# Another order of work in the opening of a fused FNet and GeGLU kernel, and other places for three kinds of transfer in its last stage

## The chip, the cores and the metric

The kernel runs on one core of a Trainium2 chip. The core has a matrix engine (TensorE, PE in the profile; its weight loads are shown apart as PEld), a vector engine (VectorE, DVE), a scalar engine (ScalarE, ACT), a general engine (GpSimd, POOL) and SyncE (SP), which only issues transfers. Each of the first four works through its own instructions in the order in which they were written. The metric is the device time of one execution in microseconds; lower is better.

## The reference

```
xn = (x - mean) / sqrt(var + eps)             # x: 2048 rows of 448, statistics by row
a  = xn @ Wd_re.T ;  b = xn @ Wd_im.T         # hidden transform, 448 x 448
s  = Ws_re @ a - Ws_im @ b                    # sequence transform, 2048 x 2048
h  = gelu(xn @ w_gate) * (xn @ w_up)          # 448 x 1792 each
g  = silu(h @ w_down)                         # 1792 x 448
y  = x + s * g
```

All inputs are fp32. The kernel splits each fp32 operand into a high part (rounded to the format that the matrix engine takes, fp32r) and a low part (the difference), and adds three products: high by high, high by low, low by high. So nearly every operand costs a copy by ScalarE (the high part) and a subtraction by VectorE (the low part).

## The kernel before

The 2048 rows are 4 chunks of 512, a chunk is 4 row tiles of 128. The kernel has four stages.

**Opening.** For each row tile: VectorE takes the statistics (`one`, L154: bn_stats and bn_aggr), ScalarE and VectorE turn them into a factor (`root` and `newton`, L158 to L170), VectorE normalizes (`norm`, L172), TensorE turns the tile over (`turn_mm`, four transposes into one PSUM bank of two that take turns), and `turn_split` (L196) empties that bank: ScalarE copies the high part (L199), ScalarE copies the plain fp32 values to `xf` (L201, kept for the Strassen sums), VectorE subtracts to get the low part (L202). Between these TensorE multiplies the first weight blocks (`first`, L544, with 256 columns at a time; `gu_mm`, L353; `gateup`) and multiplies back (`down`, L406 to L433). `act` (L382) is the Gelu and the product: Gelu by ScalarE (L386), product by VectorE (m, L389), high part by ScalarE (h, L390), low part by VectorE (l, L391). Four sums per pair of chunks and side (`combine`, L207) prepare the Strassen products: for chunks 0 and 1 on VectorE, for chunks 2 and 3 on GpSimd. `t_places` and `v_places` split those sums, `prep_s` splits the summed weights that `sums_s` made on GpSimd.

**Strassen units** (`strassen`, L447; its products at L438 and L445): 24 units of matmuls, two weight blocks by two chunks each, with the multiplications back (`send`) in between; VectorE and ScalarE work through lists (`preps`) at four places of a unit. In the first units these lists also hold what is left of the splits of the chunks' sums.

**Hidden transform** (`hid_mm`): 16 row tiles; 14 of the results are kept as sums of halves (`TS`, seven blocks of 448 columns each), and four of these are also written to device memory as `td`.

**Last stage**, the loop at the end of `fnet_geglu`: for each of eight pairs of output row tiles 14 units of 14 matmuls (`seven`, L1113 and L1116, seven products by two) and two plain units (`plain`, L1128 to L1130). Two kept tiles are exchanged in each pair: unit 0 and unit 1 free a place each, and the loop loads the tiles that units 12 and 13 need into them, in four parts each, at the units that `LOAD_AT` names (L1180). `load_c` fetches the sequence matrices five units ahead, on SP (L1005) and with a second part on POOL (L1006); VectorE sums (L1012, L1013) and splits them (ScalarE L142, VectorE L143). In unit 13 and after it `gather` takes the seven products out of PSUM into the buffer `cc`: ScalarE one (L1136), VectorE seven (L1138 to L1144). In the next pair VectorE multiplies by the gate (L1151), POOL adds x by an accumulating transfer (L1153), and SP stores the two result tiles from `cc` at the units of `STORE_AT` (L1155). The last pair has its own places for loads (`LAST_AT`), and VectorE does all its additions (L1193 to L1229).

Everything is placed by hand: the order of the source is the order on each engine and each queue, and the framework adds the waits that the data, the buffers and the PSUM banks need. What an engine or a queue waits for holds up all that is written behind it there.

Of the kernel before, what the change touches and what calls it, by code (L numbers as in the profile page):

```python
# [10 lines left out]
AF = mybir.ActivationFunctionType  # L11
# [34 lines left out]
def fnet_geglu(ctx: ExitStack, tc: tile.TileContext, x, ca, ct, cp, et, wgu, wd, out):  # L46
# [102 lines left out]
    def stats(c, k0, n):  # L149
        st = const.tile([P, 4, 6], F32, name=f"st{c}_{k0}", tag="st", bufs=2)  # L150
        mv = const.tile([P, 4, 2], F32, name=f"mv{c}_{k0}", tag="mv", bufs=3)
        sd = const.tile([P, 4, 4], F32, name=f"sd{c}_{k0}", tag="sd", bufs=3)

        def one(i):  # L154
            nc.vector.bn_stats(st[:, i], xr[c][:, k0 + i, :D])
            nc.vector.bn_aggr(mv[:, i], st[:, i])

        def root():  # L158
            r, t, w = sd[:, :n, 0], sd[:, :n, 1], sd[:, :n, 2]
            nc.scalar.activation(t, mv[:, :n, 1], AF.Sqrt, bias=epst)  # L160
            nc.vector.tensor_scalar(w, mv[:, :n, 1], EPS, -0.5, op0=ALU.add, op1=ALU.mult)
            nc.vector.tensor_scalar_mul(sd[:, :n, 3], mv[:, :n, 0], -1.0)

        def newton():
            r, t, w = sd[:, :n, 0], sd[:, :n, 1], sd[:, :n, 2]
            nc.vector.reciprocal(r, t)

            nc.vector.tensor_mul(t, r, r)
            nc.vector.tensor_mul(t, t, w)
            nc.vector.scalar_tensor_tensor(r, t, 1.5, r, op0=ALU.add, op1=ALU.mult)  # L170

        def norm(i, eng=nc.vector):  # L172
            v = xr[c][:, k0 + i]
            if eng is nc.scalar:
                eng.activation(v, v, AF.Identity, bias=sd[:, i, 3:4])
                eng.activation(v, v, AF.Copy, scale=sd[:, i, 0:1])
            else:
                eng.tensor_scalar(
                    v, v, mv[:, i, 0:1], sd[:, i, 0:1], op0=ALU.subtract, op1=ALU.mult
                )  # L180

        return one, root, newton, norm
# [13 lines left out]
    def turn_split(c, k, pt):  # L196
        sl = slice(k * P, (k + 1) * P)
        h, l = [cols_of(xs(c, lo), c, sl) for lo in range(2)]
        nc.scalar.activation(h, turned(pt, c), AF.Copy)  # L199
        for i, v in enumerate(xf[c]):  # L200
            nc.scalar.activation(v[:, :, sl], pt[:, 3 * i :] if i else pt[:, : v.shape[1]], AF.Copy)  # L201
        nc.vector.tensor_sub(l, turned(pt, c), h)  # L202
# [313 lines left out]
    with tc.manual_schedule():  # L516
# [82 lines left out]
        one, root, newton, norm = stats(1, 0, 4)  # L599
        one(0)  # L600
        one(1)
        turn_split(*t2)
        turn_split(*t3)
        one(2)
        one(3)
# [6 lines left out]
        first(1, half[1], ("hh", "hl"))  # L612
        t0, t1 = turn_mm(1, 0), turn_mm(1, 1)
        first(1, half[1], ("lh", "last"))
        turn_split(*t0)
        turn_split(*t1)
# [4 lines left out]
        d_low()  # L621
# [5 lines left out]
        turn_split(*t2)  # L627
        turn_split(*t3)
        one(1)
        m0, h0, l0 = act(0, 0, pgs[0])  # L630
        m1, h1, l1 = act(1, 0, pgs[1])
# [8 lines left out]
        l1()  # L640
        newton()
        norm(0)
        norm(1)
        gu_mm(pg[0], ws[0], 0, 1, half[1], True)
# [8 lines left out]
        turn_split(*turn_mm(2, 0))  # L653
# [15 lines left out]
        comb = combine(0, 0, nc.vector) + combine(0, 1, nc.vector)  # L669

        def turn2(k):
            turn_split(*turn_mm(2, k))
            if k == 1:
                l0()
            comb.pop(0)()
# [6 lines left out]
        one(1)  # L682
        m1()
        h1()
        one(2)
        one(3)
        root()
        l1()
        newton()
        norm(0)  # L690
        norm(1)

# [3 lines left out]
        for c in (2, 3):  # L696
# [4 lines left out]
            m0, h0, l0 = gateup(0, c, ws[0])  # L701
            if c == 2:
                turn = lambda k: turn_split(*turn_mm(3, k))
                between = [
                    lambda: (m0(), h0(), norm(2)),
                    lambda: (l0(), norm(3), turn(0), comb.pop(0)()),
                    lambda: (turn(1), comb.pop(0)()),
                    lambda: (turn(2), comb.pop(0)()),
                ]
                between1 = [lambda: (turn(3), comb.pop(0)())]  # L710
            else:
                t_split = t_places(0)
                between = [
                    lambda: (m0(), v_split(2)),
# [4 lines left out]
                between1 = [lambda: v_split(0), lambda: v_split(3)]  # L719
            down(0, c - 1, wdn, between)  # L720
            if c == 2:
                nws[0], steps = prep_s(0, s_raw)
                for f in steps:
                    f()
            m1, h1, l1 = gateup(1, c, ws[1], between1)
            m1()
            if c == 2:
                h1()
                l1()
                comb.pop(0)()  # L730
                v_split = v_places(0)
                v_split(1)
# [54 lines left out]
        for gi in range(1, len(GROUPS)):  # L787
# [7 lines left out]
            for bi, (i, p) in enumerate(zip((0, 1, 1, 0), sides)):  # L795
                preps = [[], [], [], []]
                if gi == 1 and bi == 0:
                    for f in combine(1, 1, nc.gpsimd) + combine(1, 0, nc.gpsimd):
                        f()
                    tsp, vsp = t_places(1), v_places(1)  # L800
                    preps[0].append(lambda: vsp(3))
                    preps[3].append(lambda: (vsp(1), tsp(1)))
                if gi == 1 and bi == 1:
                    for n, f, k in ((0, tsp, 2), (1, vsp, 2), (2, tsp, 0), (3, vsp, 0)):
                        preps[n].append(lambda f=f, k=k: f(k))
                if gi == 1 and bi == 2:
                    tsp(3)
# [290 lines left out]
        LOAD_AT = 2, 3, 4, 5, 6, 7, 8, 9  # L1098
        LAST_AT = 2, 2, 3, 4, 5, 6, 7, 8
        STORE_AT = 5, 8  # L1100
# [208 lines left out]
```

## Time and profile before

| | |
|---|---|
| median of 3 runs (lowest to highest) | 774.27 us (773.34 to 774.31) |
| profiled execution: time, span | 775.69 us, 773.9 us |
| mean granted TensorE clock | 0.999 |
| busy, share of the span: PE / PEld / DVE / ACT / POOL | 99% / 89% / 71% / 47% / 25% |
| matmuls | 4044 |
| moved by DMA | 170.05 MB, 220 GB/s |

The busy time of PE counts each matmul from its start to its modelled end, and successive matmuls overlap. A short stall between two of them therefore hardly shows as idle time; it shows in the distance between their starts.

### The profile page before, as it was taken

The numbers are of one execution on the slowest core, as the hardware profiler recorded it, in microseconds if no ns is written. First come the engines' busy times: TensorE is split into PE (matmuls) and PEld (weight loads), VectorE is DVE, ScalarE is ACT, GpSimd is POOL, SyncE is SP. The second block draws the span as 40 slices with busy tenths as digits, with TensorE's granted clock in tenths as the row PEclk, the third lists the DMA queues.
The fourth block names the chain that finished last, engine by engine and source line by source line (L and its number), as shares of the span: only waits on it lengthen the run. The fifth ranks groups of instructions, "written<-read, shape, count | busy, mean of one in ns | idle before, by whom it ended". The sixth has DMA issues, their size and how long they took to land.

```text
span 773.9 us, 11384 instructions
## 1 busy us (share of the span) xinstructions
PE 763.9 (99%) x4044; PEld 686.2 (89%) x4044; DVE 546.6 (71%) x937; ACT 363.7 (47%) x538; POOL 189.8 (25%) x308
## 2 busy tenths in 40 slices
PE   8999999999999999999999999999999999999997
PEld 7888888888888888888889999999899999999996
DVE  7789867555556555456452767888788797979787
ACT  3885545434444344344444585544344444434341
POOL 1109133340511511501011001223132322313130
PEclk9999999999999999999999999999999999999999
DMA  8232557994969958875979972869696969697794
GB/s 296 89 119 89 205 200 159 266 188 90 271 116 242 275 114 221 175 157 87 265 210 248 376 319 71 272 222 320 204 335 190 360 194 360 205 310 235 275 289 173
DMA packets 61370, 170.05 MB, mean 220 GB/s; under 512 B 7424, under 2 KB 40064, under 8 KB 60416
## 3 DMA queue, kind: packets, MB, share of 16 engines
q1 hardware_dynamic: 47440, 108.17, 39.6%
q0 software_dynamic: 13728, 61.02, 34.4%
q8 instruction: 32, 0.52, 0.3%
q14 instruction: 26, 0.21, 0.1%
q10 hardware_dynamic: 144, 0.11, 0.0%
HBM read 127.21 MB, written 70.91 MB: 256 GB/s over the span
## 4 chain that ended last, share of the span: by engine, by line
PE 81%; DMA 8%; DVE 7%; issue 2%; ACT 1%; SPq 0%; POOL 0%; DVEq 0%; POOLq 0%
PE x L438 23%; PE po L415 17%; PE p L1113 13%; PE ab L927 9%; PE p L1116 6%; PE x L445 4%; DMA w<-td 3%; PE gu L361 3%; DMA tmp<-ct 2%; DVE xt L143 2%; PE py L1128 1%; PE py L1130 1%; PE py L1129 1%; DMA raw<-wgu 1%; DVE e L143 1%
## 5 line engine op out<-in xcount | busy, mean ns | idle before, releaser
L438 PE MATMUL x<-xt,w 128*128 128x512 f32 x480 | 149.5, 392 | 0.0
L438 PEld LDWEIGHTS x<-xt,w 128*128 128x128 f32 x480 | 90.1, 188 | 16.1 <-DVE tmp L477 0.4
L422 ACT ACTIVATE po_out<-po 128x448 f32<-128x448 f32 x112 | 60.2, 538 | 81.0 <-PE po L415 79.8
L415 PE MATMUL po<-wd0h,hs 128*128 128x448 f32 x256 | 81.7, 366 | 0.0
L427 POOL DMA_DIRECT2D gs<-po_out x24 | 21.4, 890 | 219.0 <-ACT po_out L422 213.9
L927 PE MATMUL ab<-e,xt 128*128 128x448 f32 x288 | 68.8, 365 | 0.0
L415 PE MATMUL po<-wd,hs 128*128 128x448 f32 x288 | 66.0, 365 | 0.0
L438 PE MATMUL x<-t_v,w 128*128 128x512 f32 x216 | 60.7, 389 | 0.0
L415 PEld LDWEIGHTS po<-wd,hs 128*128 128x128 f32 x288 | 54.1, 188 | 6.6
L927 PEld LDWEIGHTS ab<-e,xt 128*128 128x128 f32 x288 | 54.1, 188 | 4.3
L415 PEld LDWEIGHTS po<-wd0h,hs 128*128 128x128 f32 x256 | 48.1, 188 | 5.0
L1006 POOL DMA_DIRECT2D raw<-sums x45 | 24.8, 551 | 98.9 <-DVE xt L143 60.0
L438 PEld LDWEIGHTS x<-t_v,w 128*128 128x128 f32 x216 | 40.6, 188 | 8.7
L415 PE MATMUL po<-wd0l,hs 128*128 128x448 f32 x128 | 46.9, 366 | 0.0
L142 ACT ACTIVATE e<-raw 128x896 fp32r<-128x896 f32 (+1 forms) x30 | 27.7, 922 | 38.1 <-DVE raw L1013 21.9
L493 ACT ACTIVATE hs<-tmp 128x512 fp32r<-128x512 f32 x24 | 15.2, 634 | 54.8 <-DVE tmp L491 54.8
L1113 PE MATMUL p<-w,e 128*128 128x448 f32 x112 | 36.9, 377 | 1.5 <-DMA w<-td 1.4
L438 PE MATMUL x<-t_lo,w 128*128 128x512 f32 x96 | 37.4, 389 | 0.0
L1113 PE MATMUL p<-t_v,wd0l 128*128 128x448 f32 x112 | 36.4, 374 | 0.0
L1006 POOL DMA_DIRECT2D tmp<-sums x39 | 21.4, 550 | 59.4 <-DVE xt L143 41.8
L142 ACT ACTIVATE e<-tmp 128x896 fp32r<-128x896 f32 (+1 forms) x22 | 19.7, 896 | 32.7 <-DVE tmp L1013 21.8
L323 DVE TENSOR_TENSOR w<-raw,w 128x512 fp32r<-128x512 f32 (+1 forms) x24 | 21.3, 889 | 18.8 <-ACT w L321 18.7
(318 smaller groups left out, 2027.4 us busy)
## 6 DMA issues: line engine op xcount, KB each, us to landing
gs<-po_out POOLq DMA_DIRECT2D x24, 896.0 KB, 8.0
sums<-ca SPq DMA_DIRECT2D x16, 896.0 KB, 9.8
sums<-ca POOLq DMA_DIRECT2D x16, 896.0 KB, 14.5
t_v<-td SPq DMA_DIRECT2D x24, 448.0 KB, 5.6
w<-td SPq DMA_DIRECT2D x24, 448.0 KB, 7.3
raw<-ct SPq DMA_DIRECT2D x45, 192.0 KB, 4.6
raw<-wgu SPq DMA_DIRECT2D x12, 640.0 KB, 6.1
tmp<-ct SPq DMA_DIRECT2D x39, 192.0 KB, 5.1
```

What stands on the lines that cost most here:

```text
L142: nc.scalar.activation(h, src, AF.Copy)
L143: nc.vector.tensor_sub(l, src, h)
L361: nc.tensor.matmul(ps[:, cols], a, xt[:, cols], start=n == 0, stop=n == len(mm) - 1)
L415: nc.tensor.matmul(po[:, :D], hs[:, a, kk * P : (kk + 1) * P], wdn[b][:, i], start=n == 0, stop=n == 5,)
L422: nc.scalar.activation(out_[0][:, kk], po[:, :D], AF.Copy)
L427: nc.gpsimd.dma_start(gv[:, 4 * c : 4 * c + 4], out_[0], accum_op=ALU.add)
L438: nc.tensor.matmul(ps, a[i], b[j], start=first and n == 0, stop=n == 2, skip_group_check=True)
L445: nc.tensor.matmul(ps, a[0], xt, start=False, stop=True, skip_group_check=True)
L927: nc.tensor.matmul(p[:, :D], a, b, start=n == 0, stop=n == len(mm) - 1)
L1006: nc.gpsimd.dma_start(v[:, 4 * P : 6 * P], sums[j][:, KS.index(k)])
L1113: nc.tensor.matmul(ps[q][:, :D], h, v, start=u % UN == 0, stop=False, skip_group_check=True)
L1116: nc.tensor.matmul(ps[q][:, :HD], l, v[:, :HD], start=False, stop=u % UN == NS - 1, skip_group_check=True,)
```

## The change

In the opening: `turn_split` can take two turned tiles. Both high copies then come first, then both subtractions, and the plain copies last; `mid` is work that is written between the subtractions and the plain copies. For a single tile `early` puts the subtraction ahead of the plain copy. The statistics of one row tile of chunk 1 are taken by ScalarE (`one.s`). The two Gelus of chunk 0 move ahead of the plain copies of chunk 1, and low parts, sums and Gelus move to other places in the order. Chunks 2 and 3 are combined by VectorE (`comb1`) in place of GpSimd. In the last stage the loads of kept tiles are issued in units 1 to 8 instead of 2 to 9, and the stores of results in units 9 and 11 instead of 5 and 8.

```diff
@@ -155,6 +155,17 @@
             nc.vector.bn_stats(st[:, i], xr[c][:, k0 + i, :D])
             nc.vector.bn_aggr(mv[:, i], st[:, i])
 
+        def one_s(i):
+
+            xi, (mean, var), q = xr[c][:, k0 + i, :D], [mv[:, i, e : e + 1] for e in (0, 1)], sd[:, i, 2:3]
+            nc.scalar.activation(tmp(0)[:, :D], xi, AF.Identity, accum_out=q)
+            nc.scalar.activation(mean, q, AF.Copy, scale=1.0 / D)
+            nc.scalar.activation(sd[:, i, 3:4], q, AF.Copy, scale=-1.0 / D)
+            nc.scalar.activation(tmp(0)[:, :D], xi, AF.Square, bias=sd[:, i, 3:4], accum_out=q)
+            nc.scalar.activation(var, q, AF.Copy, scale=1.0 / D)
+
+        one.s = one_s
+
         def root():
             r, t, w = sd[:, :n, 0], sd[:, :n, 1], sd[:, :n, 2]
             nc.scalar.activation(t, mv[:, :n, 1], AF.Sqrt, bias=epst)
@@ -193,13 +204,29 @@
     def cols_of(v, c, sl):
         return v[:, :, sl] if c % 2 == 0 else v[:, :, :, sl]
 
-    def turn_split(c, k, pt):
-        sl = slice(k * P, (k + 1) * P)
-        h, l = [cols_of(xs(c, lo), c, sl) for lo in range(2)]
-        nc.scalar.activation(h, turned(pt, c), AF.Copy)
-        for i, v in enumerate(xf[c]):
-            nc.scalar.activation(v[:, :, sl], pt[:, 3 * i :] if i else pt[:, : v.shape[1]], AF.Copy)
-        nc.vector.tensor_sub(l, turned(pt, c), h)
+    def turn_split(*turns, mid=None, early=False):
+        hl = []
+        for c, k, pt in turns:
+            sl = slice(k * P, (k + 1) * P)
+            hl.append([cols_of(xs(c, lo), c, sl) for lo in range(2)])
+            nc.scalar.activation(hl[-1][0], turned(pt, c), AF.Copy)
+        def lows():
+            for (c, k, pt), (h, l) in zip(turns, hl):
+                nc.vector.tensor_sub(l, turned(pt, c), h)
+
+        early = early or len(turns) > 1
+        if early:
+            lows()
+        if mid:
+            mid()
+        for c, k, pt in turns:
+            sl = slice(k * P, (k + 1) * P)
+            for i, v in enumerate(xf[c]):
+                nc.scalar.activation(
+                    v[:, :, sl], pt[:, 3 * i :] if i else pt[:, : v.shape[1]], AF.Copy
+                )
+        if not early:
+            lows()
 
 
     SPOT = ((0, 0), (1, 1), (1, 0), (0, 1))
@@ -597,12 +624,10 @@
         t2, t3 = turn_mm(0, 2), turn_mm(0, 3)
         first(1, half[0], ("lh", "last"))
         one, root, newton, norm = stats(1, 0, 4)
+        turn_split(t2, t3, mid=lambda: one.s(3))
         one(0)
         one(1)
-        turn_split(*t2)
-        turn_split(*t3)
         one(2)
-        one(3)
         root()
         newton()
         for i in range(3):
@@ -610,25 +635,24 @@
         norm(3, nc.scalar)
         first(0, half[1], ("hh", "lh", "hl", "last"))
         first(1, half[1], ("hh", "hl"))
+        first(1, half[1], ("lh",))
         t0, t1 = turn_mm(1, 0), turn_mm(1, 1)
-        first(1, half[1], ("lh", "last"))
-        turn_split(*t0)
-        turn_split(*t1)
+        first(1, half[1], ("last",))
+        turn_split(t0, t1)
         one, root, newton, norm = stats(2, 0, 4)
         wdn, (d_high, d_low) = prep_d(GROUPS[0], draw)
         d_high()
         one(0)
-        d_low()
         load_x(3, 0, 4)
         pg = gu_ps(0, 1)
         gu_mm(pg[0], ws[0], 0, 1, half[0], True)
         t2, t3 = turn_mm(1, 2), turn_mm(1, 3)
         gu_mm(pg[1], ws[0], 1, 1, half[0])
-        turn_split(*t2)
-        turn_split(*t3)
+        acts0 = []
+        turn_split(t2, t3, mid=lambda: acts0.extend(act(f, 0, pgs[f]) for f in range(2)))
+        d_low()
         one(1)
-        m0, h0, l0 = act(0, 0, pgs[0])
-        m1, h1, l1 = act(1, 0, pgs[1])
+        (m0, h0, l0), (m1, h1, l1) = acts0
         m0()
         h0()
         m1()
@@ -637,10 +661,10 @@
         one(3)
         root()
         l0()
-        l1()
         newton()
         norm(0)
         norm(1)
+        l1()
         gu_mm(pg[0], ws[0], 0, 1, half[1], True)
         gu_mm(pg[1], ws[0], 1, 1, half[1])
         norm(2)
@@ -650,7 +674,7 @@
         pg = gu_ps(1, 1)
         for g in range(2):
             gu_mm(pg[g], ws[1], g, 1, slice(0, 512))
-        turn_split(*turn_mm(2, 0))
+        turn_split(turn_mm(2, 0))
         h0()
         xp = [dram.tile([P, 2, 1024], F32, name=f"xp{p}") for p in range(2)]
 
@@ -666,13 +690,14 @@
         spill(0)
         s_raw = load_s(GROUPS[1][0], 1)
         sums_s(s_raw, nc.gpsimd)
-        comb = combine(0, 0, nc.vector) + combine(0, 1, nc.vector)
+        comb = combine(0, 1, nc.vector) + combine(0, 0, nc.vector)
 
         def turn2(k):
-            turn_split(*turn_mm(2, k))
+            turn_split(turn_mm(2, k), early=k == 3)
             if k == 1:
                 l0()
-            comb.pop(0)()
+            if k == 1:
+                comb.pop(0)()
 
         between = [lambda k=k: turn2(k) for k in (1, 2, 3)]
         down(0, 0, wdn, between)
@@ -680,15 +705,16 @@
         one, root, newton, norm = stats(3, 0, 4)
         one(0)
         one(1)
+        one(2)
         m1()
         h1()
-        one(2)
         one(3)
+        l1()
         root()
-        l1()
         newton()
         norm(0)
         norm(1)
+        comb.pop(0)()
 
         nws = [None, None]
 
@@ -698,34 +724,43 @@
                 draw = load_d(GROUPS[1], a_st[:, 2304:])
             else:
                 s_raw2 = load_s(GROUPS[1][1], 1)
-            m0, h0, l0 = gateup(0, c, ws[0])
             if c == 2:
-                turn = lambda k: turn_split(*turn_mm(3, k))
+                pg = gu_ps(0, c)
+                for g in range(2):
+                    gu_mm(pg[g], ws[0], g, c, slice(0, 512))
+                first = []
+            else:
+                m0, h0, l0 = gateup(0, c, ws[0])
+            if c == 2:
+                turn = lambda k: turn_split(turn_mm(3, k))
                 between = [
-                    lambda: (m0(), h0(), norm(2)),
-                    lambda: (l0(), norm(3), turn(0), comb.pop(0)()),
+                    lambda: norm(2),
+                    lambda: (norm(3), turn(0), comb.pop(0)()),
                     lambda: (turn(1), comb.pop(0)()),
-                    lambda: (turn(2), comb.pop(0)()),
+                    lambda: (turn(2), comb.pop(0)(), first.extend(act(0, 2, pg)), first[0]()),
                 ]
-                between1 = [lambda: (turn(3), comb.pop(0)())]
+                between1 = [lambda: (turn(3), first[1](), steps[0](), first[2](), steps[1]())]
             else:
                 t_split = t_places(0)
                 between = [
-                    lambda: (m0(), v_split(2)),
+                    lambda: (m0(), v_split(2), comb.pop(0)()),
                     lambda: (h0(), t_split(1)),
                     lambda: (l0(), t_split(2)),
                     lambda: (t_split(0), t_split(3)),
                 ]
-                between1 = [lambda: v_split(0), lambda: v_split(3)]
+                comb1 = combine(1, 1, nc.vector) + combine(1, 0, nc.vector)
+                between1 = [lambda: v_split(0), lambda: (v_split(3), comb1.pop(0)(), comb1.pop(0)())]
             down(0, c - 1, wdn, between)
             if c == 2:
                 nws[0], steps = prep_s(0, s_raw)
-                for f in steps:
-                    f()
             m1, h1, l1 = gateup(1, c, ws[1], between1)
             m1()
-            if c == 2:
+            if c == 3:
+                comb1.pop(0)()
+                comb1.pop(0)()
+            else:
                 h1()
+                comb.pop(0)()
                 l1()
                 comb.pop(0)()
                 v_split = v_places(0)
@@ -795,15 +830,16 @@
             for bi, (i, p) in enumerate(zip((0, 1, 1, 0), sides)):
                 preps = [[], [], [], []]
                 if gi == 1 and bi == 0:
-                    for f in combine(1, 1, nc.gpsimd) + combine(1, 0, nc.gpsimd):
-                        f()
                     tsp, vsp = t_places(1), v_places(1)
-                    preps[0].append(lambda: vsp(3))
-                    preps[3].append(lambda: (vsp(1), tsp(1)))
+                    preps[0].append(lambda: (comb1.pop(0)(), vsp(3)))
+                    preps[2].append(lambda: comb1.pop(0)())
+                    preps[3].append(lambda: comb1.pop(0)())
                 if gi == 1 and bi == 1:
-                    for n, f, k in ((0, tsp, 2), (1, vsp, 2), (2, tsp, 0), (3, vsp, 0)):
+                    comb1.pop(0)()
+                    for n, f, k in ((0, vsp, 1), (1, tsp, 1), (2, tsp, 2), (3, vsp, 2), (3, tsp, 0)):
                         preps[n].append(lambda f=f, k=k: f(k))
                 if gi == 1 and bi == 2:
+                    vsp(0)
                     tsp(3)
                 if bi == 0:
                     if gi == 1:
@@ -1095,9 +1131,9 @@
                 nc.sync.dma_start(gx[t], gv[:, 2 * j + t])
 
 
-        LOAD_AT = 2, 3, 4, 5, 6, 7, 8, 9
+        LOAD_AT = 1, 2, 3, 4, 5, 6, 7, 8
         LAST_AT = 2, 2, 3, 4, 5, 6, 7, 8
-        STORE_AT = 5, 8
+        STORE_AT = 9, 11
         GX_AT = 13, 15
         LAST_GX = 11, 12
```

## The prediction

> **What bounds the kernel now.** I read the page first, then TensorE's timeline, then the waits of the stretches where its starts spread out.
>
> ```profile
> span 773.9 us, 11384 instructions
> PE 763.9 (99%) x4044; PEld 686.2 (89%) x4044; DVE 546.6 (71%) x937; ACT 363.7 (47%) x538; POOL 189.8 (25%) x308
> ```
>
> TensorE bounds it, busy for 99% of the span. No matmul is added or removed, so the change can only take stalls between matmuls away, or put new ones in. They sit in the opening and in the last stage:
>
> ```profile
> 13.93 0.60 ACT L199 ACTIVATE xt<-pt 128x512 fp32r<-128x512 f32 x1 [1.39 <-PE pt L187]
> 14.77 0.63 DVE L155 BATCH_NORM_STATS2 st<-xf 128x6 f32<-128x448 f32 x1
> 15.63 1.62 PE L556 MATMUL gu<-xt,w 128*128 128x256 f32 x12
> 16.25 1.27 DVE L202 TENSOR_TENSOR xt<-pt,xt 128x512 fp32r<-128x512 f32 x2
> 17.58 1.46 PE L556 MATMUL gu<-xt,w 128*128 128x256 f32 x10 [0.33 <-DVE xt L202]
> 18.20 0.59 DVE L155 BATCH_NORM_STATS2 st<-xf 128x6 f32<-128x448 f32 x1
> 19.04 0.30 ACT L160 ACTIVATE sd<-mv,epst 128x4 f32<-128x4 f32 x1 [3.04 <-DVE mv L156]
> 19.32 0.72 ACT L175 ACTIVATE xf<-xf,sd 128x512 f32<-128x512 f32 x1
> 20.20 1.46 DVE L178 TENSOR_SCALAR xf<-xf,mv,sd 128x512 f32<-128x512 f32 x3
> 20.84 1.13 PE L187 MATMUL pt<-ident,xf 128*128 128x128 f32 x8 [0.36 <-issue]
> 21.51 0.60 ACT L199 ACTIVATE xt<-pt 128x512 fp32r<-128x512 f32 x1 [0.53 <-PE pt L187]
> 21.73 1.43 PE L556 MATMUL gu<-xt,wd 128*128 128x256 f32 x10
> 22.63 0.69 DVE L202 TENSOR_TENSOR xt<-pt,xt 128x512 fp32r<-128x512 f32 x1 [0.97 <-ACT xf L201]
> 23.14 1.95 PE L361 MATMUL gu<-xt,w 128*128 128x256 f32 x11
> 24.35 0.53 PEld L361 LDWEIGHTS gu<-xt,w 128*128 128x128 f32 x4 [0.33 <-DVE xt L202]
> 27.64 1.28 ACT L386 ACT_TABLE_LOAD   x1
> 28.40 1.85 PEld L361 LDWEIGHTS gu<-xt,w 128*128 128x128 f32 x15 [0.32 <-DVE xt L202]
> 30.30 5.18 PE L361 MATMUL gu<-xt,wd 128*128 128x512 f32 x22
> 42.05 0.84 PE L361 MATMUL gu<-xt,w 128*128 128x512 f32 x3
> 42.51 0.68 DVE L202 TENSOR_TENSOR xt<-pt,xt 128x512 fp32r<-128x512 f32 x1
> 43.24 4.60 PE L361 MATMUL gu<-xt,w 128*128 128x512 f32 x19 [0.35 <-DVE xt L202]
> 53.66 0.42 PEld L187 LDWEIGHTS pt<-ident,xr_a 128*128 128x128 f32 x4 [0.39 <-DVE xt L202]
> 62.45 1.76 DVE L391 TENSOR_TENSOR hs<-tmp,hs 128x512 fp32r<-128x512 f32 x1 [0.70 <-ACT hs L390]
> ```
>
> A 128x256 matmul starts 0.12 us after the one before it (ten from 21.73 end their steps at 22.93), a 128x512 one 0.227. Against these steps the starts are late by 0.59 at 17.58 (twelve from 15.63 end at 17.09; the first after a stall costs another 0.10), 0.52 at 20.84, 0.24 at 23.14, 0.38 at 24.35, 0.18 when the third half begins near 27.2, 0.37 at 28.40, 0.62 at 43.24 and 0.23 at 53.66: 3.1 us. Nearly all wait for a low part (L202). The row at 22.63 shows why it is late: its high copy ended at 22.11, but it starts right behind the plain copy of the same bank.
>
> **The opening, part by part.** *Chunk 0, tiles 2 and 3.* High copies at 13.93 and, with no plain copy between, 0.50 later, done by 15.02. VectorE is free at 14.77: low parts 14.77 to 15.45 and 15.37 to 16.05. TensorE wants them at 17.09: minus 0.59, and its row runs on to 20.43 with the six matmuls that the change moves ahead of the turn.
>
> *Statistics.* VectorE loses one tile, 0.75 (18.20 to the next step), so the root comes at 18.28 for 19.04, and the first normalized tile at 19.98. TensorE arrives at 20.43: minus 0.52. ScalarE pays for it with two wide and three small activations. No row shows Square or a sum taken on the way; by the nearest rows they cost 0.60 and 0.72 plus three times 0.20 to 0.30, 1.9 to 2.2, and with another 0.30 for each of the two sums 2.8. I take 2.2: from 14.93 to 17.1, then both plain copies to 18.2, just ahead of the root; 2.8 would make TensorE 0.2 late. Their cover is ScalarE's idle 3.04.
>
> The Trainium skill, "ScalarE: Activation LUTs", section "Table sets", says that cheap functions stand in every set and names relu, copy, identity and abs, not Square; its section "What ACT_TABLE_LOAD costs" gives about 2.66 us for a switch, of it 1.38 of draining. The load at 27.64 took 1.28, and the copy before it had ended at 27.63, so the trace shows no such drain. By the page a switch there and back would cost 5.3, and the opening would lose 2.2 (an estimate) instead of gaining the 2.6 below.
>
> *Chunk 1.* Turns at 20.43, high copies 0.67 later (20.84 to 21.51): 21.10 and 21.58, done at 22.18. But only four matmuls are left behind the turns, to 21.88, so TensorE now waits 0.35 plus 0.10, in place of 0.24. Low parts at 21.73 and 22.33, done 23.02; TensorE wants them at 23.17: minus 0.38. The next turns come at 23.65, their high copies end at 25.5 (behind two plain copies and a copy of weights), low parts at 26.35; wanted at 25.94 and 26.78: minus 0.55. TensorE is at 28.6 where it was at 30.30. The Gelus with their table load run from 25.5 to 27.9, so that their bank is free at 28.6.
>
> *Chunk 2.* Everything VectorE and ScalarE do up to the low part of tile 3 moves along, and this one now precedes its plain copy, and two of the three sums between the tiles have left: done near 40.85, wanted at 41.0 (28.6 plus the 11.75 from 30.30 to 42.05, plus three matmuls, 0.68). Minus 0.62. At 53.66 the low part no longer stands behind a Gelu and a table load: minus 0.23. *Opening: 2.6 less.* Bounds: all stalls gone, 3.1; half of it, 1.3.
>
> *Chunks 2 and 3 on VectorE:* eight instructions of 0.68 (as L202 at 42.51), 5.4 us. TensorE's matmuls up to the first Strassen units hide them; without that cover the 5.4 would show. On GpSimd's queue the weight sums behind them come earlier. Against it stand instructions like the one at 62.45, 1.76 for 0.69 while GpSimd's sums ran. I take nothing.
>
> **The last stage.**
>
> ```profile
> 539.77 9.25 DMA w<-td
> 576.32 8.80 DMA w<-td
> 683.15 9.04 DMA w<-td
> ```
> ```profile
> 521.80:526.10 4.30, 4.30 (x30) 4.10 (x29) 4.23 (x9) 2.08 (x3) 1.99 (x3) 1.00 0.71 217
> 528.30:546.00 17.70, 17.70 (x115) 16.90 (x114) 11.98 (x22) 7.07 (x9) 5.30 (x9) 1.00 1.05 365
> ```
> ```profile
> 549.06 0.47 PE L1113 MATMUL p<-w,e 128*128 128x448 f32 x1 [1.13 <-DMA w<-td]
> 583.36 0.54 ACT L1136 ACTIVATE cc<-p 128x448 f32<-128x448 f32 x1 [1.93 <-DMA tmp<-sums]
> 586.62 0.29 DVE L1012 TENSOR_TENSOR tmp<-tmp 128x128 f32<-128x128 f32 x1 [0.80 <-DMA tmp<-ct]
> 591.34 1.08 DVE L143 TENSOR_TENSOR e<-tmp,e 128x896 fp32r<-128x896 f32 x1
> 592.85 0.26 PE L1116 MATMUL p<-w,e 128*128 128x224 f32 x1
> 761.01 0.53 ACT L1136 ACTIVATE cc<-p 128x448 f32<-128x448 f32 x1
> 761.75 0.61 DVE L1138 TENSOR_TENSOR cc<-cc,p 128x448 f32<-128x448 f32 x1
> 770.45 0.69 DVE L1229 TENSOR_TENSOR cc<-cc,tmp 128x224 f32<-128x224 f32 x2
> ```
> ```profile
> L999 SPq DMA_DIRECT2D tmp<-x x1: 332/332/332, 758.0 to 758.0; - x1
> DMA to landing us min/median/max: 4.6/4.6/4.6
> ```
>
> In the second, third and sixth pair the last part of the second kept tile lands after unit 13 wants it: by the starts of its matmuls (the first in the row at 549.06) TensorE loses 1.39, 0.54 and 0.34, 2.27 in all. The transfers are full meanwhile (share 1.05) and the queue holds 9 us. Issued a unit earlier, with neither store ahead of it on SP's queue, it lands in time: minus 2.27.
>
> But the gather writes into what the stores read. The first store moves behind the load that the row at 586.62 waited for, which landed at 586.5. Without two stores ahead of it (229 KB each, 0.63 at 365 GB/s), and with the queue starting a unit earlier into a share of 0.71 (0.29 of 4.3 us, 1.25), that load lands at 584.0, the store itself at 584.7, where ScalarE's first write came at 583.36; behind ScalarE's copy and three steps VectorE (and the second store) puts the row of 586.62 at 587.1, 0.5 later. From there VectorE runs without a gap to 592.42, and TensorE, now 0.54 earlier, would want it at 592.31: of the 0.43 of slack to 592.85, 0.6 are lacking. The same reckoning takes 0.6 in the second pair; in the others, whose queues are shorter, I take nothing. At the end the first store comes behind the load issued at 758.0, landed 762.6: minus the two stores, plus itself, 762.0, and the copy of 761.01 waits for it by 1.0. VectorE's chain of additions has no gap from 761.75 to the end, so about 0.9 is lost there. *Last stage: minus 2.3, plus 0.6, 0.6 and 0.9: minus 0.2.*
>
> The Trainium skill, "DMA: Bandwidth & Descriptors", section "Anatomy of one DMA", fits one transfer on the other path with 2.0 us plus its bytes over 436 GB/s, an estimate of 2.5 for a store: it would land before the gather, and the last stage would keep its 2.3. The full queue above speaks against it.
>
> **Sum:** minus 2.6 minus 0.2, 2.8 less. The profiled execution took 775.69 (span 773.9 and 1.8 around it), 1.4 over the median of 774.27; the pieces are differences within it, so I take them off the median: **771.5**.
>
> **Rivals.** *The stores never delay the gather* (they land like other transfers of a drained queue): the opening's 2.6 and the whole 2.3, 769.4. For it: three pairs show stalls, the rest of the queue drains within a unit of 13. *VectorE becomes the bound behind the opening*: from 56 to 62.4 it has a low part, two splits of weights, a product, a sum and a low part in a row, and the last is wanted at 63.0; a 1.76 for 0.69 there, as at 62.45, costs 0.5 to 1.5. With it 772.8. Against it: GpSimd's sums, which stretched that row, are gone. *Square needs another table:* two loads of 1.28 put the root 2.5 later, less 0.45 of slack: 773.6. *The stores hold up every gather, slower than before:* one mechanism, at L1136 and L1140. If the earlier start fills no idle time, each store lands 1.25 later: pairs two and three lose 1.85 each, the four others 1.25 less a slack of 0.43, half of which I count, 1.6, and the end 0.9. That is 6.2 against 2.27 and 2.6: 775.6. It decides from 4.9 on. For it: the queue is full to unit 13; against it: the share of 0.71.
>
> **How the numbers follow.** Forecast 45%, stores free 22%, VectorE the bound 17%, stores everywhere 8%, Square 4%, other 4%. About 0.2%, 1.55 us, can be told from no change: faster is under 772.72, slower over 775.82. Faster takes 41 of the forecast's 45, the 22 and 7 of the 17: 0.70; slower half of the 8 and some of the rest: 0.06; within 0.24. The likeliest case alone spans 770.6 to 772.8; 8 in 10 lie from 769.0 to 773.8.
>
> **What would show it.** Each L202 of the paired turns right behind its high copy; TensorE's first 128x512 matmul near 28.6 and its third weight block of chunk 2 near 40.3, no stall behind it; the first Strassen matmul 2.6 earlier; a new wait near 22. No wait on td in unit 13. If L1136 waits for a transfer of `out` and the first units of the next pair start late, the give-back is right; if not, the first rival. A table load before 19 or a VectorE wait near 62 would make the forecast wrong.

## The result

The changed kernel takes 778.32 us (median of 7 runs, 776.00 to 780.89) against 773.87 for the kernel before (773.05 to 774.42): the ratio is 1.0055, with a 95% interval from 1.0038 to 1.0073. It is slower by 4.45 us, where 771.5 was forecast, and its times spread over 4.9 us where those of the kernel before spread over 1.4.

The profiled execution of the changed kernel took 776.26, near the lowest of its seven runs. From its page, the first lines and the chain that ended last:

```profile
span 774.4 us, 11390 instructions
PE 763.8 (99%) x4044; PEld 686.5 (89%) x4044; DVE 544.5 (70%) x943; ACT 365.9 (47%) x545; POOL 178.0 (23%) x300
...
PE 93%; DVE 4%; DMA 1%; issue 1%; ACT 1%; SPq 0%; DVEq 0%; ACTq 0%
```

TensorE is as busy as before, so the time must again be looked for between its starts. Lines from 158 on have moved by 11 to 36: L199, L201, L202 are now L212, L225, L215, the gather's L1136 and L1140 are L1172 and L1176, the stores' L1155 is L1191.

**The opening did what it was meant to.** Rows of the timeline of the changed kernel (start, duration, engine, line, operation, and in brackets the idle time ahead of it and who ended it):

```profile
14.08 1.09 ACT L212 ACTIVATE xt<-pt 128x512 fp32r<-128x512 f32 x2 [1.40 <-PE pt L198]
14.89 1.29 DVE L215 TENSOR_TENSOR xt<-pt,xt 128x512 fp32r<-128x512 f32 x2
15.05 0.58 ACT L161 ACTIVATE tmp<-xf 128x448 f32<-128x448 f32 x1
16.08 0.67 ACT L164 ACTIVATE tmp<-xf,sd 128x448 f32<-128x448 f32 x1
16.87 0.20 ACT L165 ACTIVATE mv<-sd 128x1 f32<-128x1 f32 x1
18.48 0.30 ACT L171 ACTIVATE sd<-mv,epst 128x4 f32<-128x4 f32 x1 [0.43 <-DVE mv L156]
20.55 1.04 PE L198 MATMUL pt<-ident,xf 128*128 128x128 f32 x8
22.32 1.58 PE L388 MATMUL gu<-xt,w 128*128 128x256 f32 x11 [0.27 <-ACT xt L212]
25.57 1.28 ACT L413 ACT_TABLE_LOAD   x1
28.56 2.68 PE L388 MATMUL gu<-xt,wd 128*128 128x512 f32 x11
72.16 1.07 PE L465 MATMUL x<-xt,w 128*128 128x512 f32 x4
```

The low parts run without a pause behind the high copies, the statistics by ScalarE take 2.02 us, no table load stands beside the Square (L164), and of the eight stalls one is left, at 22.32 in place of the one at 23.14 (a new one, of 0.30, stands at 35.90). The first matmul of the Strassen units starts at 72.16; before it was this row:

```profile
74.55 1.30 PE L438 MATMUL x<-xt,w 128*128 128x512 f32 x5
```

That is 2.39 earlier, and 2.51 if both are measured from the matmul behind the second turn of chunk 0 (14.46 now, 14.34 before).

**The last stage lost more than that.** Around the gather of the third pair, on VectorE, ScalarE and TensorE:

```profile
583.18 0.62 DVE L1176 TENSOR_TENSOR cc<-cc,p 128x448 f32<-128x448 f32 x1 [1.04 <-DMA out<-cc]
583.72 0.29 DVE L1048 TENSOR_TENSOR tmp<-tmp 128x128 f32<-128x128 f32 x1
588.44 1.08 DVE L143 TENSOR_TENSOR e<-tmp,e 128x896 fp32r<-128x896 f32 x1
```
```profile
588.72 0.38 PE L1149 MATMUL p<-w,e 128*128 128x448 f32 x1
589.58 0.37 PE L1152 MATMUL p<-w,e 128*128 128x224 f32 x1 [0.48 <-DVE e L143]
```

The third step of the gather (L1176) writes what the second store still reads and waits for it, 1.04: the store was issued at 578.61 and landed at 583.06. From there VectorE has no pause until it has split the matrices of the next pair's unit 1 (the L143 at 588.44 ends at 589.52), and TensorE waits for that split. Who waited for the stores in the changed kernel (in the kernel before nobody does):

```profile
L1191 SPq DMA_DIRECT2D out<-cc x14: 343/383/442, 538.8 to 758.4; - x14
...
who waited for it (us, times):
  DVE cc L1176: 4.9, 6
  ACT cc L1172: 1.7, 1
...
DMA to landing us min/median/max: 3.8/4.6/6.1
```

So all seven gathers that have a store ahead of them wait for it. From the first matmul of a pair to that of the next, undisturbed pairs take 35.57 (the first 35.86). The third, fourth, sixth and seventh take 36.03, 36.33, 35.84 and 36.13, together 2.05 more, and the last pair loses 1.0 at its unit 1. At the end the copy waits for the first store as well:

```profile
761.38 0.55 ACT L1172 ACTIVATE cc<-p 128x448 f32<-128x448 f32 x1 [1.72 <-DMA out<-cc]
```

```profile
770.67 0.68 DVE L1265 TENSOR_TENSOR cc<-cc,tmp 128x224 f32<-128x224 f32 x2
```

VectorE's chain behind it ends at 771.35, 40.95 after the last pair's start at 730.40. Before it ended 38.06 after it (771.14 and 733.08), so 2.9 is lost in this pair, and the 2.5 of the opening are gone and more.

### The profile page after: what moved, and what is told of

Its sections match the earlier page's. It is cut to its first block, busy times and chain, and to the rows that moved or that the text cites. A ratio compares the mean times of both kernels' runs of the same rounds, so it can differ in the third digit from the quotient of the medians.

```text
span 774.4 us, 11390 instructions
## 1 busy us (share of the span) xinstructions
PE 763.8 (99%) x4044; PEld 686.5 (89%) x4044; DVE 544.5 (70%) x943; ACT 365.9 (47%) x545; POOL 178.0 (23%) x300
## 4 chain that ended last, share of the span: by engine, by line
PE 93%; DVE 4%; DMA 1%; issue 1%; ACT 1%; SPq 0%; DVEq 0%; ACTq 0%
PE x L465 23%; PE p L1149 19%; PE po L442 17%; PE p L1152 10%; PE ab L963 9%; PE x L472 4%; PE gu L388 3%; PE gu L583 1%; PE py L1164 1%; PE py L1165 1%; DMA out<-cc 1%; PE py L1166 1%; PE warm L565 1%; DVE e L143 1%; PE pt L198 1%
```

## The experiments

All times are medians, all ratios are to the kernel before on the same chip, with the 95% interval.

| kernel | opening | loads in units | stores in units | us | ratio |
|---|---|---|---|---|---|
| changed | new | 1 to 8 | 9, 11 | 778.32 | 1.0055 (1.0038 to 1.0073) |
| opening alone | new | 2 to 9 | 5, 8 | 771.55 | 0.9970 (0.9958 to 0.9981) |
| last stage alone | old | 1 to 8 | 9, 11 | 779.81 | 1.0073 (1.0060 to 1.0087) |
| loads alone with it | new | 1 to 8 | 5, 8 | 771.42 | 0.9965 (0.9953 to 0.9977) |
| stores alone with it | new | 2 to 9 | 9, 11 | 779.26 | 1.0070 (1.0056 to 1.0085) |
| stores read elsewhere | new | 1 to 8 | 9, 11 | 771.19 | 0.9965 (0.9952 to 0.9978) |
| last pair's stores old | new | 1 to 8 | 9, 11; last pair 5, 8 | 776.24 | 1.0029 (1.0014 to 1.0043) |
| first store old | new | 1 to 8 | 5, 11 | 776.30 | 1.0035 (1.0022 to 1.0048) |
| stores between | new | 1 to 8 | 7, 9 | 771.06 | 0.9961 (0.9948 to 0.9973) |

### Which part loses

Four kernels split the change. The opening alone:

```diff
-        LOAD_AT = 1, 2, 3, 4, 5, 6, 7, 8
+        LOAD_AT = 2, 3, 4, 5, 6, 7, 8, 9
...
-        STORE_AT = 9, 11
+        STORE_AT = 5, 8
```

> The changed kernel with the loads of kept tiles back in units 2 to 9 and the stores back in units 5 and 8, so the opening alone is changed. Theory A (the opening gives its 2.4 us, as the changed profile's first Strassen matmul at 72.2 for 74.6 says, and the loss sits in the last stage): 873.9 is not in question, 773.9 minus 2.4 gives 771.5, and the first Strassen matmul again starts near 72.2. Theory B (arriving 2.4 us earlier, or the moved sums, disturbs what follows, and the last stage's edit is innocent): 776 or more.

It took 771.55. The opening's gain is real, 2.57 us, and arriving earlier disturbs nothing: every pair from the second on takes 35.56 to 35.59 us.

The last stage alone, on the kernel before:

```diff
-        LOAD_AT = 2, 3, 4, 5, 6, 7, 8, 9
+        LOAD_AT = 1, 2, 3, 4, 5, 6, 7, 8
...
-        STORE_AT = 5, 8
+        STORE_AT = 9, 11
```

> The kernel before with the loads of kept tiles in units 1 to 8 and the stores in units 9 and 11, so the last stage alone is changed. Theory A (late stores hold up the gather): 778.3 plus the 2.4 of the opening, 780.7, with the same stalls at L143 in unit 1 of a pair and a late copy of the gather at the end. Theory B (the last stage's edit is innocent): 771.5 to 774.

It took 779.81, 5.7 more than the kernel before, with 5.7 and 1.7 us of waits for the stores at L1140 and L1136. Theory B is out. Then the two edits of the last stage one at a time, on the changed kernel:

```diff
-        STORE_AT = 9, 11
+        STORE_AT = 5, 8
```

> The changed kernel with the stores alone back in units 5 and 8; loads stay in units 1 to 8. Theory A (the stores' place costs, the loads' does not): 773.9 minus 2.4, minus up to 2.3 for the waits for td in unit 13: 769.2 to 771.5, no wait of the gather for a transfer of out. Theory C (it is the earlier loads that crowd the queue for the units behind): 776 to 778.

```diff
-        LOAD_AT = 1, 2, 3, 4, 5, 6, 7, 8
+        LOAD_AT = 2, 3, 4, 5, 6, 7, 8, 9
```

> The changed kernel with the loads alone back in units 2 to 9; the stores stay in units 9 and 11. Theory A: as slow as the changed kernel, 776 to 780, the gather waits for the stores. Theory C (the earlier loads do it): 771.5.

They took 771.42 and 779.26. The stores' place carries the whole loss, the loads' place none of it: theory C is out. The waits for the line of the stores, with the old loads and the late stores:

```profile
who waited for it (us, times):
  ACT cc L1172: 5.3, 2
  DVE cc L1176: 3.2, 4
```

### The wait or the traffic

A late store could cost in two ways: the gather waits until it has read `cc`, or its bytes push back the loads of the next pair. This kernel moves the same bytes at the same places, from a tile that nobody writes:

```diff
-                stores.append(lambda: nc.sync.dma_start(ov[:, 2 * j + t], c))
+                stores.append(lambda: nc.sync.dma_start(ov[:, 2 * j + t], ab[KP[0]][0][0].bitcast(F32)))
```

> The changed kernel, with the stores in units 9 and 11 as they are, but reading a kept tile of the hidden transform that nobody writes any more, in place of the result in cc: the same bytes at the same places of the queue, and the gather's writes to cc have no store to wait for (so rows 0 to 1791 of the output are not the result; the last two tiles are). If it is the wait for the store's reading of cc: 771 to 772, pairs of 35.6 us each, the last pair's chain ends 37.6 to 38.1 after the pair's start. If it is the traffic of late stores, which pushes the next pair's loads back: 776 or more, the same stalls at L143 in unit 1.

It took 771.19, with 35.57 for every pair after the first. Nobody waits for the stores, and their landing takes no less time than in the changed kernel:

```profile
who waited for it (us, times):
busy tenths in 40 slices 0000000000000000000000000000000000000000
DMA to landing us min/median/max: 3.8/5.1/6.3
```

So it is the wait. The traffic of late stores costs nothing that can be measured.

### Where in the stage, which store, from when on

The stores of the last pair alone back in their old units:

```diff
-                if u in STORE_AT and stores:
+                if u in (STORE_AT if j < NK // 2 - 1 else (5, 8)) and stores:
```

> The changed kernel with the stores of the last pair alone in units 5 and 8; the six pairs before it store in units 9 and 11. If the end of the kernel is set by the last store that the gather waits for (the chain of additions ended 40.1 to 41.0 after the last pair's start, for 37.6 to 38.1 with the stores in units 5 and 8): 2.3 to 2.9 less than the changed kernel's 778.3, 775.4 to 776.0, and the rest, 4 to 4.5, stays in pairs two to seven. If the end is late for another reason: 778.3.

776.24, 2.1 less than the changed kernel. The copy at the end follows ScalarE's work before it again:

```profile
759.48 0.63 ACT L142 ACTIVATE t_v<-raw 128x512 fp32r<-128x512 f32 x1 [1.19 <-PE p L1152]
760.02 0.53 ACT L1172 ACTIVATE cc<-p 128x448 f32<-128x448 f32 x1
```

The other 4.8 us (776.24 to 771.42) stay, with a spread from 773.6 to 778.1 over ten runs. In the traced execution, at 774.99, they are 3.6: 2.1 in the pairs before (1.5 of it in the fourth) and 1.5 in the last pair, of which 1.0 at its unit 1.

The first store alone back:

```diff
-        STORE_AT = 9, 11
+        STORE_AT = 5, 11
```

> The changed kernel with the first store of a pair back in unit 5, the second in unit 11. ScalarE's copy of the gather waits for the first, VectorE's third step for the second. If the second alone sets VectorE's chain (it lands 2.4 to 2.8 after the first, and the third step comes 1.3 to 1.9 after the copy): most of the loss stays, 775.5 to 778. If it is the first that carries the loss: 771.4 to 773.

776.30: the second store, by VectorE's third step, keeps 4.9 of the 6.9 us (776.30 and 778.32 against 771.42). Seven times that step waits for it, 5.0 us together. The intervals of this kernel and of the one before it in the table overlap a little with that of the changed kernel, so the 2.1 and the 4.9 are rough shares.

Places between the old and the changed ones:

```diff
-        STORE_AT = 9, 11
+        STORE_AT = 7, 9
```

> The changed kernel with the stores in units 7 and 9, between the old places (5 and 8) and the changed ones (9 and 11). With the old places the second store lands 2.7 us before VectorE's third step of the gather, with the changed ones 2.0 after where that step would stand; one unit is 2 to 2.4 us of issue. If the landing follows the issue: the second store lands just ahead of the third step, no wait, or one of a few tenths in some pairs: 771.2 to 772.5. If any later store costs: 774 or more.

771.06, the lowest median of all, though its interval covers the 771.4 of the old places. Places between these and the changed ones were not run. One short wait is left in its trace:

```profile
who waited for it (us, times):
  DVE cc L1176: 0.2, 1
...
DMA to landing us min/median/max: 4.2/6.4/8.4
```

### Whether the kernel before always waits for td

> The kernel before once more, one look: does TensorE always wait for td in unit 13? If the three waits (2.27 us) belong to this kernel: they are there again and the execution takes 775 to 776. If they belong to the one profiled execution, which lay 1.4 over the median: fewer or none, 773 to 774.5.

It took 772.96. The group of matmuls that waited, on the page of the first execution and of this one:

```profile
L1113 PE MATMUL p<-w,e 128*128 128x448 f32 x112 | 36.9, 377 | 1.5 <-DMA w<-td 1.4
```
```profile
L1113 PE MATMUL p<-w,e 128*128 128x448 f32 x112 | 36.4, 374 | 0.0
```

None of the three waits came back, and the span is 2.7 shorter (771.2 for 773.9). Of the seven profiled kernels with loads in units 2 to 9 (the kernel before twice, and five of the experiments, those on the opening among them), two show such a wait; of the seven with loads in units 1 to 8, none. Two against none is too few to say that the earlier loads remove it; what the runs do show is that it belongs to some executions and not to all. How much of it is in the median this one execution, 0.8 below the median of 773.78, cannot say; the loads alone can: with the stores in their old places, early loads take 771.42 and old loads 771.55, a difference too small to be told from nothing.

### What carries the opening

Three kernels undo one edit each, on the kernel with the opening alone (771.55). The statistics back on VectorE:

```diff
-        turn_split(t2, t3, mid=lambda: one.s(3))
+        turn_split(t2, t3)
         one(0)
         one(1)
         one(2)
+        one(3)
```

> The kernel with the opening alone changed (loads in units 2 to 9, stores in units 5 and 8), but the fourth row tile's statistics of chunk 1 back on VectorE. By the forecast's step the root comes 0.75 us later and TensorE, which now reaches the turn of chunk 1 some 0.35 after its data, loses 0.4 to 0.5: first 512-column matmul at 29.0 for 28.6, time 772.0. If the statistics were not worth what the step says (slack elsewhere): 28.6 and 771.5.

772.46, ratio 0.9984 (0.9975 to 0.9993), 0.9 more. TensorE waits ahead of the turn of chunk 1:

```profile
21.31 1.07 PE L198 MATMUL pt<-ident,xf 128*128 128x128 f32 x8 [0.40 <-ACT xf L187]
```

From the matmul behind the second turn of chunk 0 to the first with 512 columns it takes 14.68 for 14.13, so the trace shows 0.55. The 0.9 of the medians is less sure: the intervals of the two kernels overlap, and in this kernel's profiled execution a wait for `td` took another 0.96.

Each plain copy right behind its high copy (which also puts ScalarE's statistics and the two Gelus of chunk 0 behind plain copies again):

```diff
+    def plain_copies(c, k, pt):
+        sl = slice(k * P, (k + 1) * P)
+        for i, v in enumerate(xf[c]):
+            nc.scalar.activation(v[:, :, sl], pt[:, 3 * i :] if i else pt[:, : v.shape[1]], AF.Copy)
...
             nc.scalar.activation(hl[-1][0], turned(pt, c), AF.Copy)
+            plain_copies(c, k, pt)
...
-        for c, k, pt in turns:
-            sl = slice(k * P, (k + 1) * P)
-            for i, v in enumerate(xf[c]):
-                nc.scalar.activation(
-                    v[:, :, sl], pt[:, 3 * i :] if i else pt[:, : v.shape[1]], AF.Copy
-                )
```

> The kernel with the opening alone changed, but each plain copy again right behind the high copy of its tile, ahead of the low parts (where the changed order put the low parts first). By the forecast's steps this order is worth 0.59 in chunk 0, 0.38 and 0.55 in chunk 1 and up to 0.85 in chunk 2: the first Strassen matmul 1.5 to 2.1 later than 71.9, time 773.0 to 773.6. If the two engines do not get in each other's way on a bank: 771.5, as before.

774.36, ratio 1.0009 (1.0000 to 1.0018): the gain is gone, and the first Strassen matmul comes 2.46 later (74.37 for 71.91), more than the 1.5 to 2.1 expected. In chunk 1 VectorE's low parts wait for the plain copies again, and TensorE waits for the high copy and the low parts:

```profile
22.48 0.69 DVE L221 TENSOR_TENSOR xt<-pt,xt 128x512 fp32r<-128x512 f32 x1 [0.97 <-ACT xf L210]
```
```profile
22.99 1.97 PE L388 MATMUL gu<-xt,w 128*128 128x256 f32 x11 [0.69 <-ACT xt L217]
...
74.37 0.84 PE L465 MATMUL x<-xt,w 128*128 128x512 f32 x3
```

The loss is not spread as expected. In chunk 0 the low parts wait too, but TensorE, which wants them near 17.1, does not wait for them:

```profile
14.92 0.69 DVE L221 TENSOR_TENSOR xt<-pt,xt 128x512 fp32r<-128x512 f32 x1 [0.26 <-ACT xf L210]
15.90 0.69 DVE L221 TENSOR_TENSOR xt<-pt,xt 128x512 fp32r<-128x512 f32 x1 [0.29 <-ACT xf L210]
```

So the 0.59 there comes from another edit: `turn_split` now stands ahead of the statistics of chunk 1, two of which had kept VectorE from these low parts until 16.25 in the kernel before. By the starts of TensorE's matmuls the plain copies cost 0.34 at the turn of chunk 1 (VectorE, behind its late low parts, takes the statistics later), 0.9 and 0.55 in chunk 1, 0.25 at 37.74 and 0.37 in chunk 2.

The sums of chunks 2 and 3 by GpSimd, at the same places of the order:

```diff
-                comb1 = combine(1, 1, nc.vector) + combine(1, 0, nc.vector)
+                comb1 = combine(1, 1, nc.gpsimd) + combine(1, 0, nc.gpsimd)
```

> The kernel with the opening alone changed, but the eight sums of chunks 2 and 3 by GpSimd, at the same places of the order. The forecast took nothing for this edit: 771.5, VectorE's rows no longer 0.69 but up to 1.8 while GpSimd's sums run, no new wait of TensorE. If VectorE's 5.4 us of sums cost something: less than 771. If the stretched rows cost the 0.5 to 1.5 of the rival: 772 to 773.

777.25, ratio 1.0036 (1.0022 to 1.0050): 5.7 us more, far outside every expectation. Its trace, at 775.07 the lowest of its four runs, shows 4.5 of them. GpSimd, VectorE and TensorE there, and a table by stretches (length; busy time and count of PE, PEld, DVE, ACT, POOL; granted clock, DMA share, GB/s):

```profile
57.97 1.62 POOL L249 TENSOR_TENSOR raw<-po_out,raw 128x512 f32<-128x512 f32 x1
59.66 1.49 POOL L250 TENSOR_TENSOR po_out<-po_out,xf 128x512 f32<-128x512 f32 x1
61.23 1.62 POOL L251 TENSOR_TENSOR xf<-xf,po_out 64x512 f32<-64x512 f32 x1
```
```profile
58.45 1.55 DVE L354 TENSOR_TENSOR w<-raw,w 64x384 fp32r<-64x384 f32 x1
60.03 1.67 DVE L418 TENSOR_TENSOR hs<-tmp,hs 128x512 fp32r<-128x512 f32 x1
61.62 2.17 DVE L350 TENSOR_TENSOR w<-raw,w 128x896 fp32r<-128x896 f32 x1
63.72 0.67 DVE L416 TENSOR_TENSOR tmp<-tmp,gu 128x512 f32<-128x512 f32 x1
```
```profile
65.11 0.47 PE L442 MATMUL po<-wd0h,hs 128*128 128x448 f32 x1 [2.26 <-ACT hs L417]
```
```profile
65.00:67.40 2.40, 2.24 (x8) 1.72 (x9) 2.31 (x4) 2.11 (x5) 0.00 (x0) 0.89 0.67 256
67.40:70.40 3.00, 3.00 (x10) 2.67 (x9) 2.41 (x5) 1.72 (x5) 2.65 (x4) 0.52 0.00 0
```

With the sums on VectorE the same rows are 0.56, 0.69 and 1.08 long and the product (L416) starts at 60.19. While GpSimd adds, VectorE falls behind by 3.5, ScalarE's copy of the product comes late, TensorE stands still for 2.3, and then its clock is granted at half for 3 us: ten matmuls where the other kernel has fifteen. The first Strassen matmul starts at 76.41 for 71.91, 4.5 later; no trace shows where the other 1.2 us of the median go.

## Why the prediction was wrong

**The opening, minus 2.6: right**, in its sum (2.57 alone, 2.51 by the positions) and in nearly every step. The low parts of chunk 0 were put at 14.77 and 15.37 and came at 14.89 and 15.50; ScalarE's statistics at 2.2, they took 2.02; the root at 18.28 (18.48), the turn at 20.43 (20.55), the new wait near 22 at 0.45 (0.43 and the 0.10 behind it), the first matmul of 512 columns near 28.6 (28.56), the third weight block of chunk 2 near 40.3 (40.55). A wait of 0.30 at 35.90, for a product of the Gelu, was not foreseen. With the plain copies between, the other edits of the opening gain nothing (2.8 lost); without the statistics on ScalarE 0.5 to 0.9 are lost. These are not shares of the 2.6, since together they are more than the whole. One reading was too broad: from the row at 22.63 the prediction explains the late low parts by the plain copies, but in chunk 0 it was VectorE's statistics, and moving the low parts ahead of them is what took away the 0.59.

**The rival of Square needing another table: out.** The Square ran at 16.08, and the next table load is the one of the Gelu, at 25.57. The Trainium skill, "ScalarE: Activation LUTs", section "Table sets", had left this open, since it does not name Square among the functions that every set has; the trace shows that here it needs no load.

**The sums on VectorE, "I take nothing": right, but for less than the whole reason.** The prediction weighed VectorE's 5.4 us against the stretched row at 62.45, and then saw VectorE as a possible bound at 56 to 62.4. VectorE ran its rows there at their short lengths, so that rival is out too. But the edit is more than hidden work: in this order it saves 5.7 us by the medians and 4.5 in the traces, because GpSimd's sums in that place bring about just the rival's stall, with a halved clock behind it.

**The last stage, minus 0.2: wrong, by 7 us.** The mechanism was in the forecast, the wait of L1140 and L1136 for the stores and no gap on VectorE from there to the next pair's unit 1. For the two pairs that were reckoned it gave 0.6 each, and TensorE lost 0.46 and 0.75 there; the row of 586.62 was put at 587.1 and came, on the old scale (3.85 later than the new one in this pair), at 587.57. The store that decided was the second, which the prediction names only in passing: on the old scale the first landed at 583.97, earlier than the 584.7 reckoned, and VectorE's third step waited for the second, which landed at 586.91. Three terms failed:

- *"Minus 2.27" for the waits for td.* They were seen in one profiled execution, which the prediction itself put 1.4 over the median, and it then took them off the median all the same. The kernel before, profiled again, has none; nor has the kernel with the opening alone, with the old loads. Off the median this term is about nothing: 771.42 against 771.55.
- *"In the others, whose queues are shorter, I take nothing."* The wait does not need a long queue. In the changed kernel the stores land after 4.6 us (median) instead of 6.6, but they are issued so late that this is not enough: three of the other pairs lost 0.27, 0.55 and 1.0.
- *"About 0.9 is lost there", at the end.* It was 2.9 in the trace, with the 1.0 of the last pair's unit 1 in it, and about 2.1 of the median comes back when the last pair's stores go back alone. The store was reckoned to be issued right behind a load that the kernel before issued 24.9 us after the last pair's start. That load came 26.7 after it, in a pair whose unit 1 was already 1.0 late, and the store at 27.1.

With these sizes the sum for the traced execution is 774.3 minus 2.5, plus 2.05 in the pairs, plus 2.9 at the end: 776.7, and it took 776.3. The median is 2 above it, and where those 2 go is not shown, since no trace shows a median execution of the changed kernel itself; the stores-alone kernel, traced at 779.25, lost 1.08, 1.73, 0.82, 1.38 and 1.16 in five pairs and 2.4 in the last (40.09 against 37.64 in the opening alone), so the same waits can be that large.

The rival of the stores holding up every gather, at 775.6 and with a chance of 8%, came nearest: every gather waited. Its prices did not hold (it had 1.85 for each of two pairs that lost 0.46 and 0.75 in the trace), and its reason, that the earlier start fills no idle time, was not tested. What kept its time low was the credit of 2.27, which it shared with the forecast: without it its own price of 6.2 leads to 774.27 minus 2.6 plus 6.2, 777.9, near the measured 778.32, in part by luck. The Trainium skill, "DMA: Bandwidth & Descriptors", section "Anatomy of one DMA", spoke for the other side: from its fit, made for transfers issued by GpSimd, the prediction had an estimate of 2.5 us for a store. No store behind a filled queue landed in that (3.8 to 6.1); the last ones, into an empty queue, did (issued at 770.17, landed at 772.12).

## What to carry to other kernels

A store is not free when it is off the path: what it reads stays locked until it has landed, so its place must be reckoned back from the next write of that buffer, and the cheapest test is to let it read something else. Before a stall in one profile is booked as a gain, see whether the execution lies above the median; if it does, the stall may be what puts it there. Where two engines empty the same bank one after the other, write first the copy that leads to what TensorE waits for: without that, the other edits of this opening gained nothing.

## What the runs showed of the hardware

GpSimd's sums stretched VectorE instructions that read both operands from SBUF, the on-chip memory of the tiles (0.69 to 1.67, 1.08 to 2.17), but none that reads its second operand from PSUM, where TensorE leaves its results. In the kernel with GpSimd's sums the first row below (`x` is in PSUM) ran at 0.69 beside a sum, the second right behind it did not. In the whole trace of that kernel 33 such instructions of 128x512 with an operand in PSUM ran beside a sum of GpSimd, none longer than 0.69; of 24 with both operands in SBUF 15 took over 0.8, up to 2.83.

```profile
79.40 0.69 DVE L497 TENSOR_TENSOR tmp<-tmp,x 128x512 f32<-128x512 f32 x1 [2.03 <-PE x L465]
80.01 1.78 DVE L418 TENSOR_TENSOR hs<-tmp,hs 128x512 fp32r<-128x512 f32 x1
```
```profile
78.58 1.29 POOL L250 TENSOR_TENSOR raw<-raw,xf 128x512 f32<-128x512 f32 x1
79.95 1.29 POOL L251 TENSOR_TENSOR xf<-xf,raw 128x512 f32<-128x512 f32 x1
```

The Trainium skill, "SBUF — State Buffer", section "Who interferes with whom", states that an instruction of VectorE with two inputs in SBUF contends with one of GpSimd that reads SBUF, and that the port pair they share is an exclusive lock. The trace agrees: GpSimd's row starts first (79.95 and 80.01), and VectorE's ends 0.56 after it (81.79 and 81.23). The prediction had the stretched row of 62.45 and could have put a price on the edit by this rule.

In the same trace the clock granted to TensorE fell to half for 3.4 us (66.86 to 70.28), 1.8 us after its work had begun again behind a pause of 2.26 us. No other pause between TensorE's matmuls in the fourteen traces is longer than 1.13 us, and in no other does the clock fall between the start-up and the last matmul, so the pause is the likely cause; one case does not prove it. Of the 4.5 us, 2.4 are the pause, 0.5 the first matmuls behind it and 1.6 the halved clock.
